# Reordering the hand-over from attention to feed-forward: an earlier gate-weight load, and four gates computed before batch 1's values

## The chip, the cores and the metric

The kernel runs on one core of a Trainium2 chip. The metric is the device time of one execution in microseconds. The kernel before takes 233.49 us (median of 3 runs, 233.4 to 233.51). Profiles are of one execution; its span, 231.7 us, starts with the first instruction and is a little shorter than the device time.

The engines are named as in the profile: PE (TensorE, matmuls; PEld is its weight load), ACT (ScalarE), DVE (VectorE), POOL (GpSimd, which issues most DMAs here) and SP (which issues stores and transposes).

## The reference

For 8 batches with 8 heads, 576 positions and head size 64, attention through 32 memory slots feeds a gated feed-forward block:

```python
a   = softmax(phi)                       # over the 32 slots
k_m = einsum('bhsm,bhsd->bhmd', a, k);   v_m = einsum('bhsm,bhsd->bhmd', a, v)
x   = softmax(q @ k_m.T / sqrt(64)) @ v_m        # heads side by side: 4608 x 512
out = (silu(x @ w_gate) * (x @ w_val)) @ w_out   # d_ff = 1536
```

## The kernel before

The kernel never forms x. For each batch it multiplies the small v_m by the weights first (U = v_m times w_gate or w_val, `u_round`, L453) and then the attention weights A by U (`gv_half`, L502). So the stages of one batch are: sums of phi with k and with v (`direct`, `kv_sum`), scores and their exponentials (`scores`, L385), the softmax denominators (`z_inv`), A = E times the inverse (`norm`, L443), U for a chunk of 512 columns of d_ff, and then 24 "slots" of 128 columns by 288 positions. A slot has a gate part (two matmuls and a silu by ACT, `gv_gate`, L517) and a value part (two matmuls and a product by DVE, the closure `mul`). The product with w_out (`products`, L682) of one batch is spread over the attention stages and the slots of the next.

The order of the work is written out by hand: the kernel is recorded with a manual schedule, each engine executes its instructions in the order of the program text, and semaphores are put in where tiles depend on each other. `run`, `spread` and `take` only arrange lists of closures. PSUM's eight banks are handed out from a list (`free`, `bank`, `done`, L72 to L84): a bank that is given back goes to the end of the list, and its next owner waits until its last reader is done.

Batches 0 and 1 are a prologue, L878 to L964. They run while the inputs and weights are still arriving. All weights, k, v and q are loaded by POOL's DMA queue in the order of the text, converting from float32 to bfloat16: k and q of batches 0 and 1, v of batch 0, v of batch 1, then the weights of chunk 0 in halves of 256 columns (`load_w(which, c, half)`, where which is 0 for the gate and 1 for the value), and then whole chunks. `v_direct(b, engs)` (L360) sums phi with v for batch b in one PSUM bank and copies the result into the third part of the tile t_kT, in four copies of 64 x 64; the letters in engs say which engine makes each, "v" for DVE and "a" for ACT. U of batch b needs it. In the same way the letters of `u_half` and `u_item` say which engine brings each half of U from PSUM to SBUF, where it is also scaled.

`warm(n)` does matmuls on a constant whose result is not used; they keep PE busy while it waits. `preload_act_table_set` loads ACT's function table for silu; before it stands the table for exp and ln.

After the first half of chunk 0, the rest of the slots of both batches follow, interleaved: `g0` and `g1` are the lists of slots of batches 0 and 1, and `flush_mul(n)` does the first n value parts that are pending. A slot of the list does its gate part first and then the pending value part of the slot before. `u_item(b, c)` is U of a whole chunk.

Of the kernel before, what the change touches and what calls it, by code (L numbers as in the profile page):

```python
# [14 lines left out]
def kernel(  # L15
# [19 lines left out]
    nc = tc.nc  # L35
# [39 lines left out]
    def bank(shape, dtype, name):  # L75
        tag = free.pop(0)
        t = ps.tile(shape, dtype, tag=tag, name=name)
        held[id(t)] = tag, t
        return t

    def done(*tiles):

        for t in tiles:
            free.append(held.pop(id(t))[0])  # L84
# [3 lines left out]
    def head_pairs(x):  # L88

        return x.rearrange("h s d -> (h s d)").rearrange("(i p f) -> p i f", i=NP, p=128)  # L90
# [11 lines left out]
    def load_v(b):  # L102
        nc.gpsimd.dma_start(out=kvs[b][:, 1], in_=head_pairs(v[b]))  # L103

    def load_q(b):

        t = inp.tile([128, NS * 128], BF16, tag=f"q{Q_SLOT[b]}", bufs=1, name="t_q")
        nc.gpsimd.dma_start(  # L108
            out=t,
            in_=q[b].rearrange("h s d -> (h s d)").rearrange("(p f) -> p f", p=128),  # L110
        )
        qs[b] = t
# [15 lines left out]
    def load_w(which, c, half=None):  # L128

        src = (moe_w_gate, moe_w_val)[which]  # L130
        split = half is not None
        if not half:
            W[which, c] = wpool.tile(
                [128, 2, NP, HC] if split else [128, NP, CH], BF16,
                tag=f"W{which}{c}", name=f"W{which}{c}",
            )
        f0, n = (half * HC, HC) if split else (0, CH)
        nc.gpsimd.dma_start(  # L138
            out=W[which, c][:, half] if split else W[which, c],
            in_=src[:, c * CH + f0:c * CH + f0 + n].rearrange("(i p) f -> p i f", p=128),  # L140
        )
# [170 lines left out]
    def direct(b, which):  # L312

        p = bank([128, NP // 2, NG, M], FP32, "p_mT")
        for n in range(NP // 2):
            for j in range(JK):
                for o in range(2):
                    nc.tensor.matmul(
                        p[64 * o:64 * o + 64, n],
                        lhsT=kvs[b][:, which, 2 * n + o, j * D:(j + 1) * D],  # L320
                        rhs=masked[b][:, j, :, 2 * n + o],
                        start=(j == 0),
                        stop=(j == JK - 1),
                        tile_position=(0, 64 * o),
                    )
        return p

    def copy(eng, out, in_):
        if eng == "a":
            nc.scalar.copy(out=out, in_=in_)  # L330
        else:
            nc.vector.tensor_copy(out=out, in_=in_)  # L332
# [27 lines left out]
    def v_direct(b, engs):  # L360

        p = direct(b, 1)
        dst = kTs[b][:, 2].rearrange("p (n o m) -> p n o m", n=NP // 2, o=2)
        for x, e in enumerate(engs):
            g, o = x % 2, x // 2
            copy(e, dst[64 * g:64 * g + 64, :, o], p[64 * o:64 * o + 64, :, g])
        done(p)
        scaled.add(b)
# [13 lines left out]
    def gv_banks():  # L382
        return [bank([128, CH], FP32, f"p_{'gv'[r]}") for r in range(2)]
# [27 lines left out]
    def z_inv(b, g):  # L411

        p = gv_banks()
        lz = att.tile([128, 2, HALF], FP32, tag="lz", bufs=3, name="t_lz")
        for r in range(2):
            nc.tensor.matmul(
                p[r][:, 0:HALF], lhsT=bones, rhs=es[b, g][:, r], start=True, stop=True
            )
            nc.scalar.activation(out=lz[:, r], in_=p[r][:, 0:HALF], func=AF.Ln)
        done(*p)  # L420
        nc.scalar.activation(out=lz, in_=lz, func=AF.Exp, scale=-1.0)  # L421
        lzs[b, g] = lz
# [20 lines left out]
    def norm(b, g):  # L443
        a = att.tile([128, 2, HALF], BF16, tag=f"A{g}", name="t_A")
        nc.vector.tensor_tensor(out=a, in0=es.pop((b, g)), in1=lzs.pop((b, g)), op=ALU.mult)  # L445
        atts[b, g] = a
# [51 lines left out]
    def flush_mul(n=None):  # L498
        for _ in range(len(pend) if n is None else n):
            pend.pop(0)()  # L500

    def gv_half(b, s, which):  # L502

        jf, r = s // 2, s % 2
        c, o = jf // 4, jf % 4
        p = bank([128, CH], FP32, f"p_{'gv'[which]}")
        for g in range(NG):
            nc.tensor.matmul(  # L508
                p[:, 0:HALF],
                lhsT=Us[b, c, g][:, o // 2, which, 128 * (o % 2):128 * (o % 2 + 1)],  # L510
                rhs=atts[b, g][:, r],
                start=(g == 0),
                stop=(g == NG - 1),
            )
        return p

    def gv_gate(b, s):  # L517

        jf, r = s // 2, s % 2
        c, o = jf // 4, jf % 4  # L520
        if o == 0 and r == 0:
            hts[b, c] = hpool.tile([128, 4, S], BF16, tag=f"h{c}", name="t_h")
        gate = gv_half(b, s, 0)
        sg = work.tile([128, HALF], BF16, tag="sg", bufs=8, name="t_sg")
        nc.scalar.activation(out=sg, in_=gate[:, 0:HALF], func=AF.Silu)  # L525
        done(gate)
        dst = hts[b, c][:, o, r * HALF:(r + 1) * HALF]

        def mul():
            val = gv_half(b, s, 1)  # L530
            nc.vector.tensor_tensor(out=dst, in0=sg, in1=val[:, 0:HALF], op=ALU.mult)  # L531
            done(val)
            if o == 3 and r == 1:
                chunk_done(b, c)

        pend.append(mul)

    def gv_slot(b, s):

        n = len(pend)  # L540
        gv_gate(b, s)
        flush_mul(n)
# [282 lines left out]
    def u_item(b, c, evac="avav"):  # L825

        return lambda: u_round(b, (((0,), c, (0, 1)), ((1,), c, (0, 1))), evac)

    def u_half(b, which, c, half, evac):

        return lambda: u_round(b, ((which, c, (half,)),), evac)
# [9 lines left out]
    def run(items):  # L841
        for x in items:
            x()
# [13 lines left out]
    def gv_slots(b):  # L857
        return [lambda s=s: gv_slot(b, s) for s in range(2 * NJF)]

    def warm(n, narrow=0):  # L860


        p = bank([128, DM], FP32, "p_warm")
        x = bones.rearrange("p (a c) -> p a c", a=1)
        sizes = [1] * narrow + [4] * ((n - narrow) // 4)
        sizes += [n - sum(sizes)] if n > sum(sizes) else []
        for a in sizes:
            nc.tensor.matmul(  # L868
                p[:, 0:128 * a],
                lhsT=bones,  # L870
                rhs=x.to_broadcast([128, a, 128]) if a > 1 else bones,
                start=True,
                stop=True,
            )
        free.insert(0, held.pop(id(p))[0])
# [18 lines left out]
        phi_exp_masked(b)  # L894
    load_q(1)
    load_v(0)
    load_v(1)
    for half in range(2):
        for which in range(2):
            load_w(which, 0, half)  # L900
    for c in range(1, NCH):
        for which in range(2):
            load_w(which, c)
# [32 lines left out]
    z_inv(1, 0)  # L936
    warm(8)
    z_inv(1, 1)
    norm(1, 0)
    warm(16)  # L940
    v_direct(1, "vvvv")
    warm(8)


    g0, g1 = gv_slots(0), gv_slots(1)
    nc.scalar.preload_act_table_set("silu_and_others")
    run([u_half(0, (0,), 0, 0, "va")])
    norm(1, 1)
    run([u_half(0, (1,), 0, 0, "va"), u_half(1, (0, 1), 0, 0, "av")])
    for s in range(4):  # L950
        gv_gate(0, s)
    flush_mul(2)
    for s in range(2):
        gv_gate(1, s)
        flush_mul(1)
    run([u_half(0, (0, 1), 0, 1, "va"), u_half(1, (0, 1), 0, 1, "aa")])
    flush_mul(2)
    run(g1[2:4] + g0[4:8] + g1[4:6])
    for c in range(1, NCH):
        s = 8 * c  # L960
        run([u_item(0, c)] + g1[s - (2 if c == 1 else 3):s] + g0[s:s + 5])
        run([u_item(1, c)] + g0[s + 5:s + 8] + g1[s:s + 5])
    run(g1[-3:])
    flush_mul()  # L964
# [146 lines left out]
```

The softmax here doesn't subtract the row's maximum and nothing guards it: scores larger than these inputs give would overflow.

## Time and profile before

| engine | busy us | share of the span | instructions |
|---|---|---|---|
| PE | 222.8 | 96% | 2825 |
| DVE | 185.3 | 80% | 423 |
| ACT | 171.7 | 74% | 365 |
| POOL | 140.6 | 61% | 190 |

A line of the timeline has the start in us, the length, the engine, the line of the kernel, the operation, the tiles (written <- read), the shape, how many instructions were merged into it, and in brackets how long the engine stood idle before it and what it waited for. For PE the length is that of the last result's arrival, so successive lines overlap; the distance between starts is what a group costs. A line of the chain of work has start, length and what the time went to. A line of the groups view has the count and then busy us and mean ns of one. A line of a DMA issue has the tile, the queue, how many, the size in KB, and the time from issue to landing in us.

### The profile page before, as it was taken

How to read it: one execution, taken by the hardware profiler on the slowest of the kernel's cores; microseconds unless marked ns; L12 is line 12 of the kernel's file. 1: busy time of each engine (PE TensorE's matmuls, PEld its weight loads, DVE VectorE, ACT ScalarE, POOL GpSimd, SP SyncE). 2: the span in 40 equal slices, each digit the busy share in tenths (PEclk: the TensorE clock that was granted, in tenths of full speed). 3: DMA queues.
4: the chain of work that ended last, by engine and by line, in shares of the span. 5: the costliest groups of instructions: out<-in, count | busy, mean ns of one | idle time of the engine just before them, and what ended most of it. 6: DMA issues, size and time to landing. Idle time of an engine off the chain costs nothing.

```text
span 231.7 us, 7206 instructions
## 1 busy us (share of the span) xinstructions
PE 222.8 (96%) x2825; PEld 169.9 (73%) x2825; DVE 185.3 (80%) x423; ACT 171.7 (74%) x365; POOL 140.6 (61%) x190
## 2 busy tenths in 40 slices
PE   7997899999999999999999999999999999999993
PEld 2554576778887776878788787887788778878882
DVE  4056789999966699989997668998999899977732
ACT  2858998988547889968896658978898789677310
POOL 8422427998199059765977689464845394039291
PEclk9999999999999999999999999999999999999999
DMA  6999999999997992999199945995013502202125
GB/s 211 210 211 205 199 207 207 219 247 269 203 205 197 260 254 44 227 212 183 54 218 193 235 131 104 249 237 102 22 71 106 112 0 95 91 6 88 29 87 160
DMA packets 36674, 36.84 MB, mean 159 GB/s; under 512 B 14624, under 2 KB 31008, under 8 KB 36640
## 3 DMA queue, kind: packets, MB, share of 16 engines
q0 software_dynamic: 16272, 22.42, 52.5%
q1 hardware_dynamic: 19600, 13.18, 22.9%
q10 hardware_dynamic: 768, 0.79, 1.1%
q8 instruction: 22, 0.36, 0.6%
q14 instruction: 12, 0.10, 0.1%
HBM read 42.47 MB, written 9.44 MB: 224 GB/s over the span
## 4 chain that ended last, share of the span: by engine, by line
PE 86%; DMA 9%; POOL 2%; ACT 1%; issue 0%; DVE 0%; POOLq 0%
PE p_g L508 21%; PE p_os L720 21%; PE p_v L508 20%; PE p_oc L720 10%; DMA W<-in_moe_w_val_dram 9%; PE p_oa L720 5%; PE p_u L465 5%; PE p_kv L230 2%; PE p_g L389 1%; POOL t_kv L99 1%; POOL t_kv L103 1%; PE p_q L376 0%; POOL t_q L108 0%; ACT t_qT L330 0%; POOL W L138 0%
## 5 line engine op out<-in xcount | busy, mean ns | idle before, releaser
L531 DVE TENSOR_TENSOR t_h<-t_sg,p_v 128x288 bf16<-128x288 bf16 x192 | 82.0, 452 | 13.7 <-PE p_v L508 6.6
L508 PEld LDWEIGHTS <-t_U 128*128 128x128 bf16 x768 | 73.7, 98 | 21.6 <-issue 3.3
L525 ACT ACTIVATE t_sg<-p_g 128x288 bf16<-128x288 f32 x192 | 73.4, 423 | 17.3 <-PE p_g L508 11.4
L508 PE MATMUL p_g<-t_A,t_U 128*128 128x288 bf16 x384 | 77.0, 286 | 0.0
L508 PE MATMUL p_v<-t_A,t_U 128*128 128x288 bf16 x384 | 77.0, 286 | 0.0
L720 PEld LDWEIGHTS <-t_S 128*128 128x128 bf16 x384 | 37.5, 98 | 4.5 <-issue 0.2
L596 POOL TENSOR_TENSOR t_S<-t_h 128x512 bf16<-128x512 bf16 x17 | 19.6, 1156 | 32.9 <-DVE t_h L531 31.4
L720 PEld LDWEIGHTS <-t_h 128*128 128x128 bf16 x288 | 27.1, 98 | 8.6 <-issue 5.0
L485 ACT CAST t_U<-p_u 128x512 bf16<-128x512 f32 x51 | 27.0, 605 | 6.6 <-PE p_u L465 6.6
L720 PE MATMUL p_os<-t_T,t_S 128*128 128x256 bf16 x192 | 23.7, 273 | 0.0
L553 POOL TENSOR_TENSOR t_S<-t_S,t_h 128x512 bf16<-128x512 bf16 x17 | 19.6, 1154 | 1.3
L553 POOL TENSOR_TENSOR t_S<-t_h 128x512 bf16<-128x512 bf16 x16 | 18.4, 1151 | 0.0
L553 POOL TENSOR_TENSOR t_S<-t_h,t_S 128x512 bf16<-128x512 bf16 x16 | 18.4, 1151 | 0.0
L465 PE MATMUL p_u<-W,t_kT 64*32 64x512 bf16 (+1 forms) x416 | 15.3, 363 | 0.9 <-DVE t_kT L332 0.6
L868 PE MATMUL p_warm<-bones 128*128 128x512 bf16 x44 | 13.7, 452 | 1.7 <-DVE bones L890 1.7
L489 DVE CAST t_U<-p_u 128x512 bf16<-128x512 f32 x21 | 13.6, 684 | 1.9 <-PE p_u L465 1.9
L720 PE MATMUL p_os<-t_T,t_h 128*128 128x256 bf16 x96 | 14.8, 273 | 0.0
L445 DVE TENSOR_TENSOR t_A<-t_E,t_lz 128x576 bf16<-128x576 bf16 x16 | 11.4, 739 | 0.7 <-ACT t_lz L421 0.7
L720 PE MATMUL p_oc<-t_T,t_S 128*128 128x256 bf16 x96 | 12.0, 272 | 0.0
L720 PE MATMUL p_oa<-WO,t_h 128*128 128x256 bf16 x96 | 11.8, 273 | 0.0
L720 PE MATMUL p_oc<-WO,t_S 128*128 128x256 bf16 x96 | 11.8, 272 | 0.0
L720 PE MATMUL p_os<-WO,t_h 128*128 128x256 bf16 x96 | 11.8, 273 | 0.0
(106 smaller groups left out, 308.4 us busy)
## 6 DMA issues: line engine op xcount, KB each, us to landing
out_dram<-t_o SPq DMA_DIRECT2D x11, 512.0 KB, 3.1
t_kv<-in_k_dram POOLq DMA_DIRECT2D x8, 576.0 KB, 10.7
t_q<-in_q_dram POOLq DMA_DIRECT2D x8, 576.0 KB, 8.6
t_kv<-in_v_dram POOLq DMA_DIRECT2D x8, 576.0 KB, 14.8
t_phi<-in_phi_dram POOLq DMA_DIRECT2D x6, 576.0 KB, 8.2
out_dram<-t_o SPq DMA_DIRECT2D x10, 256.0 KB, 3.8
WO<-in_moe_w_out_dram POOLq DMA_DIRECT2D x3, 512.0 KB, 19.2
W<-in_moe_w_gate_dram POOLq DMA_DIRECT2D x2, 512.0 KB, 16.3
```

The lines of the kernel that those rows point to most:

```text
L230: nc.tensor.matmul(p[g][32 * i:32 * i + 32, 0:n], lhsT=phi_of(b, g, j, i), rhs=kvs[b][64 * g:64 * g + 64, w0:w1, i, j * D:(j + 1) * D], st ...
L445: nc.vector.tensor_tensor(out=a, in0=es.pop((b, g)), in1=lzs.pop((b, g)), op=ALU.mult)
L465: nc.tensor.matmul(p[g][32 * i:32 * i + 32, o:o + n], lhsT=kTs[b][64 * g:64 * g + 64, 2, 32 * i:32 * i + 32], rhs=w_part(w, c, i, g, halve ...
L485: nc.scalar.copy(out=t, in_=p)
L489: nc.vector.tensor_copy(out=t, in_=p)
L508: nc.tensor.matmul(p[:, 0:HALF], lhsT=Us[b, c, g][:, o // 2, which, 128 * (o % 2):128 * (o % 2 + 1)], rhs=atts[b, g][:, r], start=(g == 0) ...
L525: nc.scalar.activation(out=sg, in_=gate[:, 0:HALF], func=AF.Silu)
L531: nc.vector.tensor_tensor(out=dst, in0=sg, in1=val[:, 0:HALF], op=ALU.mult)
L553: eng.tensor_tensor(out=out, in0=x, in1=y, op=ALU.subtract)
L596: eng.tensor_tensor(out=t[:, 0], in0=A21, in1=A22, op=ALU.add)
L720: nc.tensor.matmul(mine[home][:, u], lhsT=lhs(c, m, u), rhs=rhs(c, m), start=fresh and u == 0, stop=(k == 5), skip_group_check=u == 1 or n ...
L868: nc.tensor.matmul(p[:, 0:128 * a], lhsT=bones, rhs=x.to_broadcast([128, a, 128]) if a > 1 else bones, start=True, stop=True,)
```

## The change

It rearranges the end of the prologue, in four edits:

- The first half of chunk 0's gate weights is put ahead of batch 1's values in the DMA queue.
- U of that half for batch 0 is done right after batch 1's denominators, brought out by DVE alone ("vv"). The gate matmuls of batch 0's first four slots (`early`) follow it, ahead of `v_direct(1)`. Their silus stay where `gv_gate` puts them, behind the table load; `gv_gate` takes the finished gate as an argument. `norm(1, 1)` is also earlier, and the warm matmuls are 20 units instead of 24.
- `v_direct(1)` copies with DVE and ACT in turn ("vava") instead of DVE alone.
- Of batch 1's slots, one more is done before chunk 1's U, and one fewer after it.

It is meant to give PE useful work in the time in which it waits for batch 1's values and for the first value weights.

```diff
-    def gv_gate(b, s):
+    def gv_gate(b, s, gate=None):
...
-        gate = gv_half(b, s, 0)
+        if gate is None:
+            gate = gv_half(b, s, 0)
...
     load_v(0)
+    load_w(0, 0, 0)
     load_v(1)
-    for half in range(2):
-        for which in range(2):
-            load_w(which, 0, half)
+    load_w(1, 0, 0)
+    for which in range(2):
+        load_w(which, 0, 1)
...
     z_inv(1, 1)
+    run([u_half(0, (0,), 0, 0, "vv")])
     norm(1, 0)
-    warm(16)
-    v_direct(1, "vvvv")
-    warm(8)
+    nc.scalar.preload_act_table_set("silu_and_others")
+    warm(12)
+    early = [gv_half(0, s, 0) for s in range(4)]
+    norm(1, 1)
+    warm(4)
+    v_direct(1, "vava")
+    warm(4)
...
     g0, g1 = gv_slots(0), gv_slots(1)
-    nc.scalar.preload_act_table_set("silu_and_others")
-    run([u_half(0, (0,), 0, 0, "va")])
-    norm(1, 1)
+    for s in range(2):
+        gv_gate(0, s, early[s])
     run([u_half(0, (1,), 0, 0, "va"), u_half(1, (0, 1), 0, 0, "av")])
-    for s in range(4):
-        gv_gate(0, s)
+    for s in range(2, 4):
+        gv_gate(0, s, early[s])
     flush_mul(2)
...
-    run(g1[2:4] + g0[4:8] + g1[4:6])
+    run(g1[2:4] + g0[4:8] + g1[4:7])
     for c in range(1, NCH):
         s = 8 * c
-        run([u_item(0, c)] + g1[s - (2 if c == 1 else 3):s] + g0[s:s + 5])
+        run([u_item(0, c)] + g1[s - (1 if c == 1 else 3):s] + g0[s:s + 5])
```

## The prediction

> **What bounds the kernel now.** I read the page first: TensorE (PE) is busy 96% of the span. The chain of work that ended last says in which order that comes about.
>
> ```profile
> by line: PE p_g L508 20.8%; PE p_os L720 20.6%; PE p_v L508 20.5%; PE p_oc L720 10.1%; DMA W<-in_moe_w_val_dram 8.6%; PE p_oa L720 5.3%; PE p_u L465 5.2%; PE p_kv L230 1.9%; PE p_g L389 0.7%; POOL t_kv L99 0.7%; POOL t_kv L103 0.6%; PE p_q
> ...
> 6.74 19.97 DMA W<-in_moe_w_val_dram
> 26.71 0.04 issue
> 26.75 0.52 PE p_u L465 x24
> 27.27 1.09 PE p_g L508 x8
> ```
>
> One DMA, the first half of the value weights, carries the chain to 26.71 us; from there to the end it is PE. So what happens before 26.7 matters only through what it leaves PE to do after. The timeline of PE shows that nothing loosens it there:
>
> ```profile
> 21.28 0.76 PE L318 MATMUL p_mT<-t_mphi,t_kv 128*64 128x64 bf16 x36 [0.48 <-DMA t_kv<-in_v_dram]
> ...
> 24.22 0.76 PE L318 MATMUL p_mT<-t_mphi,t_kv 128*64 128x64 bf16 x36
> 24.91 0.61 PE L868 MATMUL p_warm<-bones 128*128 128x512 bf16 x2
> 26.07 0.30 PE L465 MATMUL p_u<-W,t_kT 64*32 64x256 bf16 x8 [0.56 <-DVE t_kT L332]
> 26.75 0.52 PE L465 MATMUL p_u<-W,t_kT 64*32 64x256 bf16 x24 [0.37 <-DMA W<-in_moe_w_val_dram]
> 27.20 1.15 PE L508 MATMUL p_g<-t_A,t_U 128*128 128x288 bf16 x8
> 28.20 0.65 PE L508 MATMUL p_v<-t_A,t_U 128*128 128x288 bf16 x4
> 28.68 0.41 PE L508 MATMUL p_g<-t_A,t_U 128*128 128x288 bf16 x2
> ...
> 29.76 0.63 PE L465 MATMUL p_u<-W,t_kT 64*32 64x256 bf16 x32
> ```
>
> A pair of gate or value matmuls comes every 0.245 us (0.1225 each) from 27.20 on; the 36 between 30.32 and 34.71 take 4.39, which is 36 x 0.122. There is no slack to give a delay back, so a shift at 28.68 (batch 1's first gate) or 29.76 (the second U round) is a shift of the end.
>
> The other views are ScalarE's (ACT) and VectorE's (DVE) timeline, for the lengths of what must now be queued there, and the DMA view of single issues.
>
> ```profile
> 25.07 1.28 ACT L946 ACT_TABLE_LOAD   x1
> ...
> 28.09 1.94 ACT L525 ACTIVATE t_sg<-p_g 128x288 bf16<-128x288 f32 x6
> ```
>
> ```profile
> 25.02 0.98 DVE L332 CAST t_kT<-p_mT 64x64 bf16<-64x64 f32 x4 [0.49 <-PE p_mT L318]
> 26.44 0.48 DVE L491 TENSOR_SCALAR t_U<-p_u,t_rS 128x256 bf16<-128x256 f32 x1 [0.44 <-PE p_u L465]
> ```
>
> ```profile
> t_kv<-in_v_dram POOLq DMA_DIRECT2D x1, 576.0 KB, 18.8
> W<-in_moe_w_gate_dram POOLq DMA_DIRECT2D x1, 256.0 KB, 19.9
> ```
>
> The last two are issued at about 5.27 and 6.00, so batch 1's values land at 24.1 (PE's weight load for them starts at 24.11) and the gate half at 25.9. The value half, issued at 6.74 and landing after 20.0, is at 26.7; the second value half, issued at 12.11 and 17.3 long, at 29.4.
>
> **What the skill says.** "PSUM — Partial Sum Buffer", section "PSUM bank collisions raise a hardware error": two engines may not touch one bank and quadrant at once, two reads included, so their accesses are ordered by semaphores. No stage of the trace before has ACT and DVE alternating on one bank. "ScalarE: Activation LUTs", section "What ACT_TABLE_LOAD costs": 186 ns + 0.833 ns per element, 93 more for a pointer operand. The trace agrees: 423 ns for the silu of 288 (426), 474 for the scaled copy of 256 (493). The same page's terms price a table load at about 2.7 us; here it takes 1.28, and that is used. "DMA: Bandwidth & Descriptors", section "Queues, rings and completion order": each DMA engine works through a queue's ring in order. The landings above come in order of issue, so a swap in the queue is a swap of landings.
>
> **Part 1, the swapped load.** Gate half (256 KB) before batch 1's values (576 KB). It rates at 256 KB in about 1.3 us (the two value and gate halves behind it land at 28.1 and 29.4), so it lands at 21.23 + 1.3 = 22.5, ahead of its use at 23.2. The same three transfers are in front of the value half as before, so that stays at 26.7. Batch 1's values become the third: they land when the third lands now, 25.9. Bounds: by rate alone 26.7 - 1.3 = 25.4. I take 25.9, because a 16 KB instruction transfer (queue 8) starts at about 23.87, holds one DMA engine for some 0.95 us and delays whatever is third in line; PE's program is fetched at about the same place after the change.
>
> **Part 2, PE ahead of that.** U gate of batch 0: kT copies of batch 0 end at 23.06, so its 8 matmuls start at 23.2 instead of 26.07. DVE starts 0.37 later (26.07 to 26.44), two copies at 0.40 and 0.48 end at 24.4. Norm(1,0) moves from 23.77 to 24.4 and norm(1,1) to 25.1, both ahead of any use: nothing. Three warm matmuls fill PE meanwhile. Four gates are 8 x 0.1225 = 0.98 us and end at 25.3, one warm matmul at 25.5. This takes 0.98 us out of PE's work after 26.7: the gain the change is for. PE then stands in order before v_direct(1) and waits to 25.9; nothing else can pass it.
>
> **Part 3, "vava".** v_direct(1) starts at 26.0 (0.11 for its weights, as 24.11 to 24.22), and the first copy 0.80 later (24.22 to 25.02): 26.8. In the built program the four copies wait on one another in turn: DVE, ACT, DVE, ACT. DVE's is 222 ns; ACT's of 64 columns is 205 to 239 (the line through 372 at 256 and 595 at 512 columns, and the skill's price), I take 220. Each hand-over is some 0.03 (ACT's t_lz ends 23.74, DVE starts 23.77). 2 x 0.222 + 2 x 0.22 + 4 x 0.03 = 1.00, as long as four on DVE (0.98). So kT of batch 1 is ready at 27.8, where it was at 26.0, and U of batch 1 starts there. PE does the 8 matmuls of U value batch 0 at 26.75 and idles.
>
> **Part 4, ACT behind the table load.** ACT's order is now: copy, copy, silu, silu, U value of batch 0 (256), U gate/value of batch 1 (512), four silus. The first two silus are ready long before and wait in the queue behind the copies. Silus follow each other at (1.94 - 0.43)/5 = 0.30. From 27.7: silu 27.7, 28.0; U value 28.3 to 28.8 (0.474); U of batch 1 28.7 to 29.4 (0.68). The values of slots 0 and 1 need the first, so PE does them at 28.8 to 29.2; batch 1's first gate needs the second: 29.4 instead of 28.68. That is +0.72. So the 0.98 us saved on PE turns into idle time before 29.4: PE has only 8 + 16 + 4 matmuls to do between 26.75 and there. After it PE's order is that of before, and what it waits for (silus of slots 2 and 3 at 30.0, products by DVE at 29.9) is ready by 30.4.
>
> **Part 5, one slot moved ahead of chunk 1.** No work added. But only one slot (4 x 0.1225 = 0.49) now stands between chunk 1's U and its first gate, where two stood. U's evacuation by DVE ends 0.54 + 0.74 = 1.28 after that round starts (34.71, 35.25); PE gets there after 0.55 + 0.49 + 0.12 = 1.16. A stall of 0.12.
>
> Sum: +0.72 + 0.12 = +0.84, 234.3 us.
>
> **The rivals.** (a) The values land by rate, 25.4. Then v_direct starts at 25.5 and everything in parts 3 and 4 is 0.5 earlier: +0.23 + 0.12, 233.8, no difference that counts. For it: the delay of the third transfer hangs on one fetch. (b) The waits on ACT overlap better than I chain them (copies, silus and U start as soon as their bank is free), and PE runs through. Then the second value half bounds it: it lands at 29.4 and is needed 0.14 into the second U round, which now starts at 29.76. At most 0.5 is to be had, less the stall of 0.12: 233.1. For it: ACT's sum is made of many short pieces. Against it: ACT is 0.89 busy in that stage already and its order is fixed. (c) PE idles so much between 25.5 and 29.4 that its clock falls. "TensorE: Matmul & The Clock Gate", section "What's actually happening", gives a window of about 3.4 us at half speed after an idle one; no run here shows it (clock 1.0 throughout, with PE 0.52 busy in the microsecond at 25). An estimate from that page: up to 1.7 us more over such a window; with half of it 235.2.
>
> **The numbers.** The sum above 0.50, (a) 0.27, (b) 0.13, (c) 0.10. The bound of 0.2% is 0.47 us: 233.02 to 233.96. (a) lies within it, (b) mostly, so faster by more is 0.07, the same 0.35, slower 0.58. The range goes from below (a), 233.3, to 234.9 above the sum with hand-overs of 0.1 and a stall of 0.25 instead; left out are most of (b) and (c).
>
> **What would show it.** PE's wait for t_kv<-in_v_dram at 25.4 to 26.0, U of batch 1 waiting for t_kT, gate of batch 1 at 29.4 waiting for ACT's t_U, the second U round at 30.5, and after it no PE wait but a short one in chunk 1. If the second U round starts before 29.76, parts 3 and 4 are wrong; if PE's pairs are longer than 0.245 us, it is the clock; if the values land at 25.4, part 1 is.

## The result and the profile after

The changed kernel takes 234.38 us (median of 6 runs, 234.23 to 234.44); the kernel before, beside it, 233.46. The ratio is 1.0039, 95% interval 1.0026 to 1.0052: slower by 0.92 us. The forecast was 234.3.

The chain of work of the changed kernel, from 6 us to batch 1's first gate (start, length, what):

```profile
6.02 19.82 DMA t_kv<-in_v_dram
25.89 0.78 PE p_mT L318 x36
26.69 0.23 DVE t_kT L332
26.94 0.21 ACT t_kT L330
27.18 0.24 DVE t_kT L332
27.43 0.21 ACT t_kT L330
27.67 0.71 ACT t_sg L526 x2
28.38 0.37 ACT t_U L487
28.80 0.56 PE p_v L508 x3
29.38 0.42 PE p_g L508 x2
```

The DMA at its head is no longer the value weights but batch 1's values. Behind it stands a ladder between engines: the sums, the four copies in turn, two silus, U's evacuation. Before, one DMA was followed by PE alone.

PE's timeline of the changed kernel:

```profile
23.18 0.30 PE L465 MATMUL p_u<-W,t_kT 64*32 64x256 bf16 x8
23.41 0.82 PE L869 MATMUL p_warm<-bones 128*128 128x512 bf16 x3
24.29 1.22 PE L508 MATMUL p_g<-t_A,t_U 128*128 128x288 bf16 x8
25.35 0.38 PE L869 MATMUL p_warm<-bones 128*128 128x512 bf16 x1
25.89 0.76 PE L318 MATMUL p_mT<-t_mphi,t_kv 128*64 128x64 bf16 x36 [0.16 <-DMA t_kv<-in_v_dram]
...
27.69 0.41 PE L465 MATMUL p_u<-W,t_kT 64*32 64x256 bf16 x15 [0.29 <-ACT t_kT L330]
28.13 0.28 PE L508 MATMUL p_v<-t_A,t_U 128*128 128x288 bf16 x1
28.80 0.54 PE L508 MATMUL p_v<-t_A,t_U 128*128 128x288 bf16 x3 [0.39 <-ACT t_U L487]
29.38 0.42 PE L508 MATMUL p_g<-t_A,t_U 128*128 128x288 bf16 x2
...
30.46 0.63 PE L465 MATMUL p_u<-W,t_kT 64*32 64x256 bf16 x32
...
36.71 0.41 PE L508 MATMUL p_v<-t_A,t_U 128*128 128x288 bf16 x2
37.11 0.43 PE L508 MATMUL p_g<-t_A,t_U 128*128 128x288 bf16 x2
```

Four gates are done by 25.4, as meant. Then PE has gaps before 27.69, 28.80 and 29.38. From 26.75 to 30.46 it is busy for 2.91 of 3.71 us; before, it was busy for all 3.01 us from 26.75 to 29.76. The second U round is 0.70 late (30.46 against 29.76). The last two lines show the second loss, at chunk 1's first gate: 0.40 between starts where pairs otherwise come every 0.245, so 0.155 more. 0.70 and 0.155 make 0.85; the span grew by 0.9.

The DMA view of the two issues in the stretch 5.95 to 6.5 us of the changed kernel:

```profile
t_kv<-in_v_dram POOLq DMA_DIRECT2D x1, 576.0 KB, 19.8
W<-in_moe_w_gate_dram POOLq DMA_DIRECT2D x1, 256.0 KB, 17.2
```

Batch 1's values, issued at 6.02, land at 25.8; the gate half, issued at 5.29, at 22.5.

### The profile page after: what moved, and what is told of

Its sections match the earlier page's. It is cut to its first block, busy times and chain, and to the rows that moved or that the text cites. A ratio compares the mean times of both kernels' runs of the same rounds, so it can differ in the third digit from the quotient of the medians.

```text
span 232.6 us, 7203 instructions
## 1 busy us (share of the span) xinstructions
PE 223.0 (96%) x2824; PEld 169.4 (73%) x2824; DVE 185.6 (80%) x422; ACT 172.0 (74%) x366; POOL 140.8 (61%) x190
## 4 chain that ended last, share of the span: by engine, by line
PE 86%; DMA 9%; POOL 2%; ACT 1%; issue 0%; DVE 0%; POOLq 0%
PE p_os L721 21%; PE p_v L508 20%; PE p_g L508 20%; PE p_oc L721 10%; DMA t_kv<-in_v_dram 9%; PE p_oa L721 5%; PE p_u L465 5%; PE p_kv L230 2%; PE p_g L389 1%; POOL t_kv L99 1%; PE p_q L376 0%; POOL t_q L108 0%; ACT t_qT L330 0%; PE p_mT L318 0%; POOL t_kv L103 0%
## 5 line engine op out<-in xcount | busy, mean ns | idle before, releaser
L869 PE MATMUL p_warm<-bones 128*128 128x512 bf16 x43 | 12.9, 434 | 1.7 <-DVE bones L891 1.7
```

The costliest lines, as they stand in the source:

```text
L869: nc.tensor.matmul(p[:, 0:128 * a], lhsT=bones, rhs=x.to_broadcast([128, a, 128]) if a > 1 else bones, start=True, stop=True,)
```

## The experiments

Executions differ by some tenths of a microsecond in when batch 0's values arrive. So the main reading is the distance from v_direct(1)'s start on PE to the second U round's, beside the times. The starts and the distance are from the profiled execution of each run. The median is over 2 executions for gates_no_swap, 3 for warm_halves and 6 to 21 for the others; each interval is against the kernel before, run beside it.

| run | v_direct(1) | second U round | distance | median us | ratio to before (95%) |
|---|---|---|---|---|---|
| changed kernel | 25.89 | 30.46 | 4.57 | 234.38 | 1.0026 to 1.0052 |
| swap_only | 25.90 | 30.94 | 5.04 | 234.61 | 1.0033 to 1.0063 |
| copies_dve | 26.08 | 30.18 | 4.10 | 233.83 | 1.0006 to 1.0021 |
| silus_first | 25.97 | 30.27 | 4.30 | 234.03 | 1.0008 to 1.0025 |
| slot_back | 25.95 | 30.52 | 4.57 | 234.20 | 1.0017 to 1.0039 |
| copies_act | 25.80 | 30.09 | 4.29 | 233.89 | 1.0005 to 1.0018 |
| values_first | 25.68 | 29.53 | 3.85 | 233.66 | 0.9997 to 1.0014 |
| gates_no_swap | 29.44 | 34.38 | 4.94 | 238.94 | 1.0211 to 1.0250 |
| warm_halves | 25.64 | 30.21 | 4.57 | 234.70 | 1.0036 to 1.0086 |
| values_first_nowarm | 26.12 | 29.94 | 3.82 | 233.58 | 0.9992 to 1.0008 |
| silus4_dve | 25.89 | 29.82 | 3.93 | 233.55 | 0.9988 to 1.0005 |

In three profiled executions PE loses more time far behind the stage that was edited: 0.85 us in swap_only (the kernel before has these five matmuls without a break),

```profile
136.57 0.27 PE L720 MATMUL p_oc<-t_T,t_Q 128*128 128x256 bf16 x1
137.53 0.60 PE L720 MATMUL p_oc<-t_T,t_Q 128*128 128x256 bf16 x4 [0.69 <-issue]
```

0.29 in gates_no_swap, in the same group of matmuls (at 140.2), and 0.27 in warm_halves (before 112.59, where PE waits for the DMA of t_kT). The starts in the table don't contain this. Why it comes in these executions is not shown.

**The swap alone.** The kernel before, with one edit:

```diff
     load_v(0)
+    load_w(0, 0, 0)
     load_v(1)
-    for half in range(2):
-        for which in range(2):
-            load_w(which, 0, half)
+    load_w(1, 0, 0)
+    for which in range(2):
+        load_w(which, 0, 1)
```

> The kernel before with one part of the change alone: the first gate half is put ahead of batch 1's values in the DMA queue, everything else stays. Theory (values land as the third transfer, at 25.9, and everything behind v_direct(1) on PE and DVE follows): v_direct(1) at 25.9 to 26.0 instead of 24.22, copies of kT on DVE to 27.8, batch 0's U behind them, gates at 28.2, batch 1's first gate near 29.9, second U round near 31.0, so 234.6 to 234.8 us. Rival 1 (the queue's rate alone): v_direct(1) at 25.4, 234.1. Rival 2 (the landing is of no account, the loss of the changed kernel is made on ScalarE): 233.5.

PE's timeline of it:

```profile
25.90 0.76 PE L318 MATMUL p_mT<-t_mphi,t_kv 128*64 128x64 bf16 x36 [1.64 <-DMA t_kv<-in_v_dram]
26.59 0.61 PE L868 MATMUL p_warm<-bones 128*128 128x512 bf16 x2
27.26 0.89 PE L465 MATMUL p_u<-W,t_kT 64*32 64x256 bf16 x32
28.26 1.15 PE L508 MATMUL p_g<-t_A,t_U 128*128 128x288 bf16 x8
...
30.94 0.63 PE L465 MATMUL p_u<-W,t_kT 64*32 64x256 bf16 x32
```

The values now hold PE for 1.64 us and everything behind them follows: the second U round is at 30.94, and the median is 234.61, 1.02 us above the kernel before. The landing as the third transfer and the loss through it are shown; both rivals fall. (The profiled execution took 235.46 and is the slowest of the six; the 0.85 us at 137 us are a part of that.) The swap costs 1.18 us at the second U round, and the rest of the change earns 0.48 of it back.

**The early gates alone.** The changed kernel with the old load order:

```diff
-    load_w(0, 0, 0)
     load_v(1)
+    load_w(0, 0, 0)
     load_w(1, 0, 0)
```

> The changed kernel with the old load order (batch 1's values before the gate half): the early gates without the swap. Theory (PE's order is fixed, and v_direct(1) stands behind gates that need the gate half): U of batch 0 starts at 25.9, gates at 26.9 to 28.1, v_direct(1) at 28.4, second U round near 33.0, 236.5 to 237 us. Rival (the swap alone makes the loss): near 233.5.

PE waits 2.73 us for the gate half, with v_direct(1) behind it, although its values were there since 23.8. So the two parts need each other: in this order on PE, the gates can't go early without the swap. The loss was bigger than the 236.5 to 237 expected, 238.94 us, and a part of that is a new thing. The view by stretches (PE, PEld, DVE, ACT, POOL busy, then the granted clock, DMA share, GB/s):

```profile
24.00:25.00 1.00, 0.00 (x0) 0.00 (x0) 0.00 (x0) 0.95 (x3) 0.74 (x1) 1.00 1.43 190
...
26.00:27.00 1.00, 0.94 (x12) 0.31 (x4) 0.84 (x3) 0.11 (x1) 0.74 (x1) 1.00 1.45 195
27.00:28.00 1.00, 1.00 (x5) 0.57 (x5) 1.00 (x3) 0.00 (x0) 0.72 (x1) 0.50 1.44 200
...
30.00:31.00 1.00, 0.94 (x32) 0.69 (x27) 0.22 (x1) 0.14 (x1) 0.75 (x1) 0.80 1.24 204
```

PE's clock was halved from 27 to 30.4 us, after the wait of 2.73. The eight gate matmuls took 1.84 from their start to that of the next group, against 1.06.

**VectorE alone for the copies.**

```diff
-    v_direct(1, "vava")
+    v_direct(1, "vvvv")
```

> The changed kernel, but batch 1's value copies all by VectorE (vvvv) as before. Theory (ScalarE's order costs the time: silus and U stand behind its two copies): kT of batch 1 is ready no earlier (27.7), but the silus of slots 0 and 1 run from 26.3 on, U value of batch 0 is out at 27.9, batch 1's first gate goes at 28.9 instead of 29.38, second U round at 30.0, 233.9 to 234.0 us. Rival (only the landing of batch 1's values at 25.9 counts): 234.4 as before this edit. Second rival (alternating copies are themselves faster than four on one engine, so undoing them loses): above 234.5.

ACT's timeline of it:

```profile
26.61 0.71 ACT L526 ACTIVATE t_sg<-p_g 128x288 bf16<-128x288 f32 x2
27.62 0.47 ACT L487 ACTIVATE t_U<-p_u,t_rS 128x256 bf16<-128x256 f32 x1 [0.30 <-PE p_u L465]
28.36 0.69 ACT L487 ACTIVATE t_U<-p_u,t_rS 128x512 bf16<-128x512 f32 x1 [0.27 <-PE p_u L465]
```

The two silus now run before U is there, and ACT waits for PE, not PE for ACT. The four copies took 0.96 (alternating: 26.69 to 27.64, 0.95). The distance is 4.10 instead of 4.57, so 0.47 of the changed kernel's loss was ScalarE's queue. 233.83 us, as expected within 0.1.

**The silus ahead of the copies.**

```diff
+    for s in range(2):
+        gv_gate(0, s, early[s])
     v_direct(1, "vava")
...
-    for s in range(2):
-        gv_gate(0, s, early[s])
```

> The changed kernel with the silus of slots 0 and 1 ahead of batch 1's value copies in ScalarE's order; the alternating copies stay. Theory (ScalarE's queue order): the silus fill 26.3 to 27.0, where ScalarE stood idle, ScalarE's first copy is late by under 0.1, U value of batch 0 is out at 28.0 and U of batch 1 at 28.9; batch 1's first gate at 28.9, second U round at 30.0, 233.9 to 234.0. Rival (landing alone): 234.4. If the wait for the copy chain is the limit and not the queue, 234.4 too.

This gave a little more than half of what was expected: 0.27 of the 0.47, 234.03 us. ScalarE's first copy came at 27.23, 0.24 after VectorE's ended, where it is 0.03 in the changed kernel; the silus end at 27.21. I had expected under 0.1. The table load ended 0.2 later in this execution (26.48 against 26.29), and nothing in this order takes that up; that this is where the other 0.2 went is argued, not tested.

**The slot put back.**

```diff
-    run(g1[2:4] + g0[4:8] + g1[4:7])
+    run(g1[2:4] + g0[4:8] + g1[4:6])
...
-        run([u_item(0, c)] + g1[s - (1 if c == 1 else 3):s] + g0[s:s + 5])
+        run([u_item(0, c)] + g1[s - (2 if c == 1 else 3):s] + g0[s:s + 5])
```

> The changed kernel with the slot of batch 1 put back behind chunk 1's U (two slots between that U and its first gate, as before the change). Theory: PE no longer catches up with VectorE's evacuation there; the gap of 0.15 us between the pairs after chunk 1's first U goes, 234.2 us. Rival (the gap is given back later, or the weights of chunk 1 then bound): 234.4.

The pairs after chunk 1's U start at 36.02, 36.28, 36.52, 36.77: the gap is gone, the distance unchanged, 234.20 us. The interval overlaps the changed kernel's, so it is the trace that shows it.

**All copies by ScalarE.** silus_first and slot_back together, and

```diff
-    v_direct(1, "vava")
+    v_direct(1, "aaaa")
```

> The changed kernel with three edits: silus of slots 0 and 1 ahead of the value copies, all four copies by ScalarE (aaaa), the slot of batch 1 put back. Theory (after the landing, what counts is the length of the copy chain and ScalarE's queue): ScalarE's copies of 64 columns overlap and take 0.5 to 0.6 us where four on VectorE or alternating took 1.0; kT of batch 1 at 27.3, both U values out at 27.9, batch 1's first gate at 28.5 to 28.6, second U round at 29.6 to 29.7, 233.3 to 233.4 us, just ahead of the kernel before. Rival (ScalarE is the bound whatever the order): second U round at 30.0 or later, 233.7 or more. Rival (the landing at 25.9 alone): 234.2.

The second U round came at 30.09, not at 29.6 to 29.7, and the time is 233.89, not 233.3 to 233.4. ACT's timeline of it:

```profile
26.87 0.89 ACT L330 CAST t_kT<-p_mT 64x64 bf16<-64x64 f32 x4
```

Four copies take 0.89 there: they do not overlap (204 ns each, one every 0.23). I had carried the overlap of the 288-column silus over to them. The distance is 4.29, that of silus_first; what is gained against it is the slot. The four copies take 0.89 to 0.98 on either engine or on both in turn.

**Batch 0's values before batch 1's gates.** copies_act, and

```diff
-    flush_mul(2)
+    flush_mul(4)
     for s in range(2):
         gv_gate(1, s)
-        flush_mul(1)
```

> As copies_act, and all four value parts of batch 0 before batch 1's first gate, so that PE has work while U of batch 1 is brought out. Theory: the 0.2 us gap before batch 1's first gate closes, second U round at 29.45 to 29.55, where the second value half (landing 29.4) begins to bound: 233.1 to 233.25 us. Rival (VectorE's products, now later, hold PSUM banks): second U round or the values behind it wait for t_h, 233.4 or more.

The second U round came at 29.53, in the range expected, 0.23 ahead of the kernel before, and no product held a bank. But the median is 233.66, above the 233.1 to 233.25 expected and the same as before (0.9997 to 1.0014). The profiled execution itself took 233.46 and is the fastest of the 13. Why the others give the 0.23 away is not shown; the landing of batch 1's values lay between 25.5 and 26.1 in the profiles of this study, and this order starts its chain with it.

**Less warming.** values_first without the two single warm matmuls around v_direct(1), and a second one that also has all four silus ahead of the copies and the copies by VectorE:

```diff
     norm(1, 1)
-    warm(4)
...
-    v_direct(1, "aaaa")
-    warm(4)
+    v_direct(1, "vvvv")
```

> values_first without the two single warm matmuls around v_direct(1). Theory: PE came to v_direct(1) only 1.49 us after the first early gate, and the values land at about the same time; without the warm matmul it waits for the landing alone (25.6 to 25.9), U value of batch 0 starts at 26.7 instead of 26.8, and the second U round comes up against the landing of its value half: second U round at 29.4 to 29.5, 233.4 to 233.6 us, no more than 0.1 to 0.2 ahead of values_first. Rival (the gaps in PE's work slow its clock): clock below 1.0 in some microsecond after 26, above 234.

> values_first without those two warm matmuls, with all four silus of batch 0 ahead of the value copies and the four copies by VectorE. Theory (the copy chain takes 0.9 to 1.0 us on whatever engine; ScalarE's queue is then empty when U value arrives): U value's ScalarE half is out at 27.6, VectorE's at 28.0, and the values of batch 0 follow; second U round at 29.4 to 29.5 against its landing, as values_first_nowarm, 233.4 to 233.6. Rival (four silus delay what matters on ScalarE): 233.9.

Both times are in the range expected and both are the same as before. The U rounds of the profiled executions are later than the 29.4 to 29.5 that the range rested on (29.94 and 29.82), because the values landed at 26.08 and 25.85 and PE waited 0.48 and 0.49 for them; so the times are no support for the theory. PE's clock stayed at 1.0. No version found beats the kernel before.

**The third landing.** The changed kernel with the first warm matmuls in twice as many instructions:

```diff
-    def warm(n, narrow=0):
+    def warm(n, narrow=0, wide=4):
...
-        sizes = [1] * narrow + [4] * ((n - narrow) // 4)
+        sizes = [1] * narrow + [wide] * ((n - narrow) // wide)
...
-    warm(104)
+    warm(104, wide=2)
```

> The changed kernel with the first 104 units of warm matmuls in 52 instructions of 256 columns instead of 26 of 512, so that PE's program is 52 instructions further on at any time after and its next instruction transfer falls earlier than 23.8. Theory (an instruction transfer on one DMA engine is what makes batch 1's values land at 25.85 instead of 25.4): with the transfer at 22 to 22.5 the values land at 25.3 to 25.6; PE comes to v_direct(1) at 25.8 anyway, so the time gains at most 0.1: 234.3. Rival (another cause, such as ScalarE's table load in the same 25.0 to 26.3): landing at 25.85 as before.

Inconclusive on time. The instruction transfer moved by only 0.3 us, to 23.47, and the values landed at 25.57, 0.27 earlier. In the trace's own records the last part of the third transfer lands 2.0 to 2.2 us after the start of the instruction transfer in ten of the twelve profiles (starts from 23.47 to 24.04); in copies_dve and silus_first, with starts at 24.33 and 24.01, it doesn't (25.61 and 25.50, so 1.3 and 1.5 after). The two mostly go together; that one causes the other is argued and not shown.

## Why the prediction was right

**Part 1, the swap:** right. 25.8 for the values (25.9), 22.5 for the gate half (22.5), and swap_only shows the cost of it. Its reason for 25.9 and against 25.4, the instruction transfer, stays argued.

**Part 2, PE ahead of it:** the mechanism was right, a term was mis-sized. The gates ran 24.29 to 25.35, but PE could not have begun v_direct(1) at 25.5. In warm_halves and copies_dve the values land a little before they are wanted; there it begins 1.49 us after the first gate. In warm_halves:

```profile
24.15 1.22 PE L508 MATMUL p_g<-t_A,t_U 128*128 128x288 bf16 x8
25.20 0.38 PE L869 MATMUL p_warm<-bones 128*128 128x512 bf16 x1
25.64 0.76 PE L318 MATMUL p_mT<-t_mphi,t_kv 128*64 128x64 bf16 x36
```

The term that was off is the single warm matmul, put at 0.2: from its start to that of the sums it takes 0.44 (0.43 in copies_dve); why is not shown. In the changed kernel 1.49 us after the first gate is 25.78. So the landing as such cost 0.11, not the 0.4 that part 2 has PE waiting, and rival (a) was wrong in its sum: with a landing at 25.4 it would have been 234.3 less 0.1, not 233.8. The chance of 0.27 given to (a) so stood for nearly the same time as the likeliest case.

**Part 3, "vava":** right. The four copies in turn took 0.95 (1.00 forecast), as long as on one engine. ACT's copy took 0.206 (0.22). The order between the two engines on one PSUM bank, for which the Trainium skill, "PSUM — Partial Sum Buffer", section "PSUM bank collisions raise a hardware error", was named, is in the chain above, step by step. The rule there is for one bank and one quadrant of 32 partitions. The second copy reads partitions 0 to 63 and the third 64 to 127, and the third waited all the same: the program as built keeps the engines apart by more than that rule asks. The tile that they write is not the reason: in the kernel before, DVE (26.44) and ACT (26.47) bring the two halves of U, from two banks, into one tile side by side.

**Part 4, ScalarE's queue:** right, in the order and in the size: batch 1's first gate at 29.38 (29.4), 0.70 late (0.72). copies_dve and silus_first take a part of it away, counted from v_direct(1)'s start and so apart from the landing, which settles that it is the queue. Part 4 starts its count at 27.7, though part 3 ends at 27.8; the copies ended at 27.64, so this slip helped the sum by 0.1, by luck. The price that the Trainium skill gives for an ACTIVATE ("ScalarE: Activation LUTs", section "What ACT_TABLE_LOAD costs": 186 ns + 0.833 per element) makes an estimate of 239 ns for the copy, a sixth more than measured; the trace lists these copies as CAST.

**Part 5, the slot:** right, 0.155 (0.12).

One count was wrong without harm: between 30.32 and 34.71 the trace before has 34 gate and value matmuls, not 36. Two distances between pairs are longer than 0.245 there (0.36 and 0.34), and they are so in the changed kernel too, so nothing of the delay is given back in them.

**Rivals (b) and (c):** (b) did not happen; PE did not run through. values_first came nearest to its bound, with the U round at 29.53, but its median is 233.66, not 233.1. (c) did not happen in the changed kernel: its clock is 1.0 up to 30 us. That it can happen in this stage is shown by gates_no_swap; the stretch at half clock was as long there as (c) has it, 3.4 us, but PE was not idle all through the 3.4 us before it: it worked from 25.80 on.

So the 0.98 us of gates were moved into idle time of PE, and the way to them was paid with a later start of the chain that PE waits for next: 1.18 by the swap, of which the early gates could give back only 0.48 because ScalarE's order was made worse in the same edit. With the copies on VectorE they give back 0.94 (distance 4.10 against 5.04 in swap_only), which is still less than 1.18.

## What to carry to other kernels

When work is pulled into an idle stretch of an engine, look at what is pushed out of it: a load moved ahead makes another one later, and what counts is the whole ladder behind that one. Before splitting small copies of one PSUM bank between two engines, check that both can work at once; here they took turns, and the second engine's queue stood behind its copies. Ready work (two silus) belongs ahead of an instruction that waits, not behind it.

## What was not expected of the hardware

- Four ScalarE copies of 64 x 64 take 0.89 us, one every 0.23 at 204 ns each, while silus of 288 columns follow each other every 0.30 at 423 ns: the copies don't overlap. Length alone does not decide it: in the kernel before, four ACTIVATEs of 64 x 1152 at 1161 ns each take 4.72 us in a row, without overlap too. The cause is open.
- A wait of 2.73 us on PE was followed by half clock for about 3.4 us; one of 1.64 (swap_only) was not, in the profiled execution. Two other executions of swap_only have a mean clock of 0.99, near the 0.989 of gates_no_swap, and no trace, so it is not excluded there.
- A DMA of 16 KB for instructions, some 0.95 us long on one DMA engine, starts in the middle of this stage in every run (23.47 to 24.33). Of the 16 parts in which the changed kernel's third transfer lands, 14 are there by 24.41, and the last comes at 25.84.
